# A three-stage kernel: the residual's rows are added to the Fourier stage's terms in channel mixing, on GpSimd, instead of within the Fourier stage on VectorE and GpSimd

## The chip, the cores and the metric

The kernel runs on one core of a Trainium2 chip. A core has five engines that run side by side, each with its own queue in a fixed order: TensorE (PE) for matmuls, VectorE (DVE), ScalarE (ACT) and GpSimd (POOL) for elementwise work, and SyncE (SP), which here only issues transfers (DMAs). ACT and POOL issue transfers too. An instruction that waits holds everything behind it on its queue. The metric is the time of one execution in microseconds (us), and less is better.

## The reference

Eight heads of linear attention over 8 batches of 576 rows give x of 8 x 576 x 512. A mixing layer with gates follows, and then the part that the change touches:

```python
def _moe2_ref(x, w_ch1, w_ch2):
    X = np.fft.fft(x, axis=1)
    X = np.fft.fft(X, axis=2)
    mixed = np.real(X).astype(np.float32)
    u = x + mixed
    mu = np.mean(u, axis=-1, keepdims=True)
    var = np.mean((u - mu) ** 2, axis=-1, keepdims=True)
    un = (u - mu) / np.sqrt(var + 1e-06)
    ch = np.maximum(un @ w_ch1, 0.0) @ w_ch2
    return (u + ch).astype(np.float32)
```

`x + mixed` is the residual: the rows that went into the Fourier transform are added to the real part of its result, and channel mixing (a layer norm and two matmuls) works on the sum u.

## The kernel before, in words

The program has three stages. Stage 1 (0 to 708 us) is attention and the gated mixing; it writes the rows x to `x1d` in DRAM, in 4 pairs of images (batches) of 9 tiles of 128 rows (`NTP` = 9): 4 tiles of each image, and a fifth tile of the pair that holds the last 64 rows of both.

Stage 2, the Fourier stage, goes over the 8 images. For image n, `f_load` brings 4 tiles of x into `xtt` (4 buffers) and, once for each pair, the shared tile into `xlt`. `f_eo` (L680 on VectorE, L681 on GpSimd) forms sums and differences of mirrored rows in `eot`, `f_fold` (L687, L690, L691, L697) the same of mirrored columns, split into a high and a low part in `fht`. `f_s` transforms along the rows: TensorE `pz` (L722), then `zt` (L724 on ScalarE, L725 on VectorE). `f_d` transforms along the columns in three parts m = 0, 1, 2 (128, 128 and 64 rows): TensorE `pd` (L756), a copy `bs` on ScalarE (L761), and on VectorE `wa`, whose two halves are the difference (L762) and the sum (L763). By symmetry each half serves two output tiles, once as it is and once mirrored along the columns. `acc` then adds the halves to the rows of x in place: columns 0 to 256 on VectorE (L766), columns 257 to 511 on GpSimd (L767). The sums are stored to `ud`, one store for each tile, on ACT's queue (L773, L779) and on SP's (L780). The step function `for t in range(-3, 4 * B + 1)` interleaves the images, four steps apart.

Stage 3 is channel mixing: 9 chunks c of 4 tiles of 128 rows. `u_load` brings the tiles of a chunk from `ud` into `ua` (two buffers, L820); the loads of chunk 0 wait for the last matmul of image 3 (`st["mm", 3]`). `ln` normalizes a tile: `bn` (L832), `mv` (L833 to L835), `una` (L837), transposes (L842), and `uh` and `ul` (L844, L845). For each of 16 slices f of the hidden layer `g1` forms `ph` (L853 to L855), `hh` on ScalarE (L858) and `hl` on VectorE (L859), and `g2` multiplies them with the second weight, one slice later (L900 to L902). `g2` adds the result to `ua` (L905) and stores it. During chunk 0 the two weights of each slice are loaded as raw 64-bit words (L62, four buffers) and split: L67 and L81 on ScalarE, L69, L72 and L75 on VectorE, L82 on GpSimd. The raw loads of slices 0 and 1 wait for image 4's last matmul, those of slices 2 and 3 for image 6's.

The order of the instructions on each engine is decided by a scheduler that simulates a timeline, not by hand: instructions of stages 2 and 3 are mixed where their inputs allow it, and bn of chunk 0 and the first weight splits run within the Fourier stage.

Of the kernel before, what the change touches and what calls it, by code (L numbers as in the profile page):

```python
# [10 lines left out]
F32 = mybir.dt.float32  # L11
# [10 lines left out]
D = H * DH  # L22
# [20 lines left out]
def kernel(ctx, tc, q, k, v, mu_k, mu_r, w_k, w_v, w_r, w_ch1, w_ch2, tab_s, tab_d, out):  # L43
# [1 line left out]
    const = ctx.enter_context(tc.tile_pool(name="const", bufs=1))  # L45
    dram = ctx.enter_context(tc.tile_pool(name="dram", bufs=1, space=DRAM))
    x1d = [dram.tile([NTP, P, D], F32, name=f"x1d{p}") for p in range(NPAIR)]
    ud = [dram.tile([P, D], F32, name=f"ud{i}") for i in range(NPAIR * NTP)]

    ident = const.tile([P, P], F32, name="ident")  # L50
    make_identity(nc, ident)
# [3 lines left out]
    def after(ins, to):  # L55
        tc.add_manual_dep(
            ins.ins, to, mybir.DependencyInfo(mybir.DependencyClass.Sync, mybir.DependencyReason.DATA), reason="pace"
        )
# [522 lines left out]
    with ExitStack() as ph:  # L581
# [50 lines left out]
        ts_ = p2.tile([P, 2, 2, 4, NS], F32R, name="ts_")  # L632
        td_ = p2.tile([P, 2, 2, 2, KC], F32R, name="td_")
        alt = p2.tile([P, KC], F32R, name="alt")
        NXT = 4
        xtt = [p2.tile([P, 4, D], F32, name=f"xtt{i}") for i in range(NXT)]
        nc.gpsimd.dma_start(ts_, tab_s)
        nc.gpsimd.dma_start(td_, tab_d[:, 0 : 8 * KC].rearrange("p (a b c n) -> p a b c n", a=2, b=2, c=2))
# [100 lines left out]
        def f_d(n, m):  # L739
            p, par = divmod(n, 2)  # L740
            z = st["z", n]
            cols = slice(256, 320) if m == 2 else slice(m * P, (m + 1) * P)
            w = 64 if m == 2 else P
            o = 64 * par if m == 2 else 0
            pd = [ps.tile([P, KC], F32, tag="pd", name=f"pd{n}_{m}_{ab}", bufs=4) for ab in range(2)]
            for ab in (1, 0):
                mm = []
                for dt in range(2):
                    i = 2 * ab + dt
                    mm.append((z[:, 0, i, cols], td_[:, 0, ab, dt]))  # L750
                    mm.append((z[:, 0, i, cols], td_[:, 1, ab, dt]))
                    mm.append((z[:, 1, i, cols], td_[:, 0, ab, dt]))
                if ab == 0:
                    mm.append((z256[n % 2][:, cols], alt))
                for j, (a, b) in enumerate(mm):
                    ins = nc.tensor.matmul(pd[ab][0:w], a, b, start=j == 0, stop=j == len(mm) - 1)  # L756
            st["mm", n] = ins.ins.name
            bs = p2.tile([P, KC], F32, tag="bs", name=f"bs{n}_{m}", bufs=2)
            wa = p2.tile([P, 2, KC], F32, tag="wa", name=f"wa{n}_{m}", bufs=2)
            r = slice(o, o + w)  # L760
            nc.scalar.copy(bs[0:w], pd[1][0:w])  # L761
            nc.vector.tensor_tensor(out=wa[r, 0], in0=pd[0][0:w], in1=bs[0:w], op=ALU.subtract)  # L762
            nc.vector.tensor_tensor(out=wa[r, 1], in0=pd[0][0:w], in1=bs[0:w], op=ALU.add)  # L763

            def acc(x, a, b, e0, e1):
                e0.tensor_tensor(out=x[:, 0:257], in0=x[:, 0:257], in1=wa[r, a, 0:257], op=ALU.add)  # L766
                e1.tensor_tensor(out=x[:, 257:512], in0=x[:, 257:512], in1=wa[r, b, 255:0:-1], op=ALU.add)  # L767

            if m == 2:
                xl = st["xl", p]  # L770
                acc(xl[r], 0, 1, nc.vector, nc.gpsimd)
                if par:
                    nc.scalar.dma_start(ud[p * NTP + 4], xl)  # L773
            else:
                xt = st["xt", n]
                acc(xt[:, m], 0, 1, nc.vector, nc.gpsimd)
                acc(xt[:, 2 + m], 1, 0, nc.vector, nc.gpsimd)
                i0 = p * NTP + 5 * par
                nc.scalar.dma_start(ud[i0 + m], xt[:, m])  # L779
                nc.sync.dma_start(ud[i0 + 2 + m], xt[:, 2 + m])  # L780

        for t in range(-3, 4 * B + 1):
            for n in range(B):
# [20 lines left out]
    with ExitStack() as ph:  # L804
# [7 lines left out]
        of = out.flatten_outer_dims()  # L812
        NCH = 9
        CT = 4
        us, uT = {}, {}

        def u_load(c):
            u = ua[c % 2]
            for t in range(CT):
                ld = nc.sync.dma_start(u[:, t], ud[c * CT + t])  # L820
                if c == 0:
                    after(ld, st["mm", 3])
            us[c] = u

        def ln(c, t):
            u = us[c]
            if t == 0:
                uT[c] = ((uha, ula), (uhb, ulb))[c % 2]
            uh, ul = uT[c]
            bn = top.tile([P, 6], F32, tag="bn", name="bn", bufs=2)  # L830
            mv = top.tile([P, 2], F32, tag="mv", name="mv", bufs=2)
            nc.vector.bn_stats(bn, u[:, t])  # L832
            nc.vector.bn_aggr(mv, bn)  # L833
            nc.scalar.activation(out=mv[:, 1:2], in_=mv[:, 1:2], func=AF.Sqrt, bias=eps)
            nc.vector.reciprocal(mv[:, 1:2], mv[:, 1:2])  # L835
            un = una[t % 2]
            nc.vector.tensor_scalar(  # L837
                un, u[:, t], mv[:, 0:1], mv[:, 1:2], op0=ALU.subtract, op1=ALU.mult
            )
            pt = psa.tile([P, NK, P], F32, tag="pt", name="pt", bufs=1)  # L840
            for kt in range(NK):
                nc.tensor.transpose(pt[:, kt], un[:, kt * P : (kt + 1) * P], ident)  # L842
            cs = slice(t * P, (t + 1) * P)
            nc.scalar.copy(uh[:, :, cs], pt)  # L844
            nc.vector.tensor_tensor(out=ul[:, :, cs], in0=pt, in1=uh.bitcast(F32)[:, :, cs], op=ALU.subtract)  # L845
# [151 lines left out]
```

## Time and profile before

| what | value |
|---|---|
| median of 3 runs | 1672.5 us (1672.42 to 1673.82) |
| the profiled execution | 1676.39 us |
| its span, first to last instruction | 1674.6 us (1.8 us lie around it) |
| mean granted TensorE clock | 0.971 of full speed |
| busy: PE, DVE, ACT, POOL | 1548.0, 746.7, 594.9, 491.5 us |
| Fourier stage | about 708 to 836 us |
| chunk 0 of channel mixing | 836 to 946 us |

The time of the profiled execution is compared with a view of the same execution alone; it lies 3.9 us above the median of the runs. The share of busy time is an average over stages with different limits, so a stage is read by itself: which engine is full there, and what the others wait for. Durations of matmuls overlap, since they are pipelined.

### The profile page before, as it was taken

What the parts mean: (1) busy time and instruction counts of PE and PEld (TensorE: products, weight loads), DVE (VectorE), ACT (ScalarE), POOL (GpSimd) and SP (SyncE); (2) the same over time, 40 slices, a digit from 0 to 9 for tenths busy, and PEclk for the clock granted to TensorE, in tenths of its full rate; (3) what the DMA queues carried; (4) which work ended last, traced back from release to release, by engine and by line L of the source; (5) the groups of instructions that cost most, each with busy time, mean ns of one, the idle gap of its engine ahead of it and who ended that gap; (6) DMA issues with size and microseconds to landing.
All of it is one profiled execution on the core that took longest, in us unless ns stands there. A gap on an engine that the chain in (4) does not pass through costs nothing.

```text
span 1674.6 us, 19835 instructions
## 1 busy us (share of the span) xinstructions
PE 1548.0 (92%) x7560; PEld 1313.2 (78%) x7560; DVE 746.7 (45%) x1342; ACT 594.9 (36%) x1120; POOL 491.5 (29%) x532
## 2 busy tenths in 40 slices
PE   2497999899989999987887999999999999999998
PEld 2476899788879888776765888888888888888886
DVE  7966544645365442199999312212221313131211
ACT  4673666566556564233445111111111111111110
POOL 4464663646365555265445000000000000000000
PEclk9598999999999999988999999999999999999999
DMA  7521322222212101435454101001010101010000
GB/s 196 164 83 51 85 56 68 64 56 70 69 51 63 58 13 51 170 110 196 167 192 157 51 0 41 11 1 50 1 51 1 50 1 51 0 51 1 26 0 26
DMA packets 117863, 108.91 MB, mean 65 GB/s; under 512 B 54760, under 2 KB 91752, under 8 KB 117512
## 3 DMA queue, kind: packets, MB, share of 16 engines
q1 hardware_dynamic: 107736, 84.37, 17.1%
q10 hardware_dynamic: 8064, 14.68, 2.4%
q0 software_dynamic: 1968, 8.60, 1.4%
q8 instruction: 59, 0.97, 0.2%
q14 instruction: 36, 0.29, 0.1%
HBM read 79.31 MB, written 28.31 MB: 64 GB/s over the span
## 4 chain that ended last, share of the span: by engine, by line
PE 66%; DVE 12%; issue 10%; POOL 4%; ACT 4%; DMA 3%; SPq 1%; POOLq 0%; ACTq 0%; DVEq 0%
PE ph L853 6%; PE ph L855 6%; PE pc L900 6%; PE ph L854 6%; PE pc L902 6%; PE pc L901 6%; PE pv L469 3%; PE pv L470 3%; PE pv L471 3%; PE pk L438 3%; PE pk L439 3%; PE pk L440 3%; DVE xm L416 2%; PE pr L454 1%; PE pr L455 1%
## 5 line engine op out<-in xcount | busy, mean ns | idle before, releaser
L859 DVE SCALAR_TENSOR_TENSOR hl<-ph,hh 128x512 fp32r<-128x512 f32 x144 | 99.2, 689 | 443.8 <-ACT hh L858 443.8
L858 ACT ACTIVATE hh<-ph 128x512 fp32r<-128x512 f32 x144 | 85.9, 597 | 515.3 <-PE ph L855 515.3
L884 POOL DMA_INDIRECT out_dram<-ua,rev x16 | 15.7, 979 | 732.0 <-DVE ua L905 731.6
L902 PE MATMUL pc<-w2h,hl 128*128 128x512 f32 x576 | 222.9, 393 | 8.2 <-DVE hl L859 8.2
L900 PE MATMUL pc<-w2h,hh 128*128 128x512 f32 x576 | 226.5, 393 | 3.9 <-ACT hh L858 3.9
L901 PE MATMUL pc<-w2l,hh 128*128 128x512 f32 x576 | 224.8, 390 | 0.0
L416 DVE SCALAR_TENSOR_TENSOR xm<-dt,omu,xb 128x63 f32<-128x63 f32 (+4 forms) x224 | 115.7, 566 | 83.2 <-POOL xr_lo L425 35.0
L438 PE MATMUL pk<-xk_hi,wk_hi 128*128 128x384 f32 x384 | 131.0, 350 | 12.4 <-ACT xk_hi L424 11.4
L446 POOL TENSOR_TENSOR kk_lo<-h,kk_hi 128x384 fp32r<-128x384 f32 x96 | 98.8, 1033 | 148.6 <-ACT h L445 130.7
L902 PEld LDWEIGHTS pc<-w2h,hl 128*128 128x128 f32 x576 | 107.6, 188 | 35.3 <-DVE hl L859 11.6
L439 PE MATMUL pk<-xk_lo,wk_hi 128*128 128x384 f32 x384 | 131.4, 343 | 0.2 <-POOL xk_lo L425 0.2
L900 PEld LDWEIGHTS pc<-w2h,hh 128*128 128x128 f32 x576 | 108.1, 188 | 29.9 <-ACT hh L858 6.5
L853 PE MATMUL ph<-uha,w1h 128*128 128x512 f32 x320 | 127.7, 401 | 2.8 <-ACT w1h L81 2.8
L440 PE MATMUL pk<-xk_hi,wk_lo 128*128 128x384 f32 x384 | 130.1, 340 | 0.0
L855 PE MATMUL ph<-uha,w1l 128*128 128x512 f32 x320 | 127.3, 398 | 1.2 <-POOL w1l L82 1.2
L854 PE MATMUL ph<-ula,w1h 128*128 128x512 f32 x320 | 126.8, 396 | 0.0
L901 PEld LDWEIGHTS pc<-w2l,hh 128*128 128x128 f32 x576 | 108.2, 188 | 23.6
L469 PE MATMUL pv<-wv,kk_hi 128*128 128x512 f32 x288 | 113.1, 394 | 0.6 <-ACT sgt L458 0.6
L470 PE MATMUL pv<-wv,kk_hi 128*128 128x512 f32 x288 | 112.9, 394 | 0.0
L471 PE MATMUL pv<-wv,kk_lo 128*128 128x512 f32 x288 | 112.4, 393 | 0.0
L853 PE MATMUL ph<-uhb,w1h 128*128 128x512 f32 x256 | 100.9, 397 | 0.0
L855 PE MATMUL ph<-uhb,w1l 128*128 128x512 f32 x256 | 100.0, 391 | 0.0
(206 smaller groups left out, 3178.6 us busy)
## 6 DMA issues: line engine op xcount, KB each, us to landing
raw<-in_moe_w_ch_dram SPq DMA_DIRECT2D x32, 512.0 KB
x1d<-sgt ACTq DMA_DIRECT2D x36, 256.0 KB
ua<-ud SPq DMA_DIRECT2D x36, 256.0 KB
kt<-in_k_dram SPq DMA_DIRECT2D x32, 256.0 KB
xtt<-x1d SPq DMA_DIRECT2D x8, 1024.0 KB
vt<-in_v_dram SPq DMA_DIRECT2D x60, 128.0 KB
qtT<-in_q_dram SPq DMA_DIRECT2D x8, 512.0 KB
qtB<-in_q_dram SPq DMA_DIRECT2D x8, 512.0 KB
```

The lines of the kernel that those rows point to most:

```text
L438: nc.tensor.matmul(pk, wh, xk_hi[:, kt], start=kt == 0, stop=False)
L439: nc.tensor.matmul(pk, wh, xk_lo[:, kt], start=False, stop=False)
L440: mm = nc.tensor.matmul(pk, wl, xk_hi[:, kt], start=False, stop=kt == NK - 1)
L469: nc.tensor.matmul(pv, kk_hi[f][:, ts], wv_hi[f // 2][:, f % 2], start=f == 0, stop=False)
L470: nc.tensor.matmul(pv, kk_hi[f][:, ts], wv_lo[f // 2][:, f % 2], start=False, stop=False)
L471: mm = nc.tensor.matmul(pv, kk_lo[f][:, ts], wv_hi[f // 2][:, f % 2], start=False, stop=f == NF1 - 1)
L853: nc.tensor.matmul(ph_, w1h[f][:, kt], uh[:, kt], start=kt == 0, stop=False)
L854: nc.tensor.matmul(ph_, w1h[f][:, kt], ul[:, kt], start=False, stop=False)
L855: nc.tensor.matmul(ph_, w1l[f][:, kt], uh[:, kt], start=False, stop=kt == NK - 1)
L900: nc.tensor.matmul(a, hh[:, cs], w2h[f], start=f == 0, stop=False)
L901: nc.tensor.matmul(a, hh[:, cs], w2l[f], start=False, stop=False)
L902: nc.tensor.matmul(a, hl[:, cs], w2h[f], start=False, stop=f == NF2 - 1)
```

## The change

The Fourier stage no longer adds the rows of x. `f_d` stores `wa` as it is, both halves in one transfer, to new buffers in DRAM: `wad` for m = 0 and 1 (128 x 2 x 258, 258 KB each), `wal` for m = 2 (64 rows of it). All 24 stores are on SP's queue. In channel mixing `u_load` brings the tile of x from `x1d` into `ua` and the `wa` that belongs to it into a new tile `wl` (4 buffers); `u_add`, called at the head of `ln`, adds the two halves to the rows on GpSimd. A `wa` of m = 0 or 1 serves two tiles and is loaded twice. `xtt` has 3 buffers instead of 4, the loads of chunk 0 wait for image 1's last matmul instead of image 3's, and the buffer for the descriptors of transfers that GpSimd issues is set to 4096 bytes.

```diff
--- before.py
+++ after.py
@@ -45,7 +45,9 @@
     const = ctx.enter_context(tc.tile_pool(name="const", bufs=1))
     dram = ctx.enter_context(tc.tile_pool(name="dram", bufs=1, space=DRAM))
     x1d = [dram.tile([NTP, P, D], F32, name=f"x1d{p}") for p in range(NPAIR)]
-    ud = [dram.tile([P, D], F32, name=f"ud{i}") for i in range(NPAIR * NTP)]
+
+    wad = [[dram.tile([P, 2, KC], F32, name=f"wad{n}_{m}") for m in range(2)] for n in range(B)]
+    wal = [dram.tile([P, 2, KC], F32, name=f"wal{p}") for p in range(NPAIR)]
 
     ident = const.tile([P, P], F32, name="ident")
     make_identity(nc, ident)
@@ -632,7 +634,7 @@
         ts_ = p2.tile([P, 2, 2, 4, NS], F32R, name="ts_")
         td_ = p2.tile([P, 2, 2, 2, KC], F32R, name="td_")
         alt = p2.tile([P, KC], F32R, name="alt")
-        NXT = 4
+        NXT = 3
         xtt = [p2.tile([P, 4, D], F32, name=f"xtt{i}") for i in range(NXT)]
         nc.gpsimd.dma_start(ts_, tab_s)
         nc.gpsimd.dma_start(td_, tab_d[:, 0 : 8 * KC].rearrange("p (a b c n) -> p a b c n", a=2, b=2, c=2))
@@ -762,22 +764,10 @@
             nc.vector.tensor_tensor(out=wa[r, 0], in0=pd[0][0:w], in1=bs[0:w], op=ALU.subtract)
             nc.vector.tensor_tensor(out=wa[r, 1], in0=pd[0][0:w], in1=bs[0:w], op=ALU.add)
 
-            def acc(x, a, b, e0, e1):
-                e0.tensor_tensor(out=x[:, 0:257], in0=x[:, 0:257], in1=wa[r, a, 0:257], op=ALU.add)
-                e1.tensor_tensor(out=x[:, 257:512], in0=x[:, 257:512], in1=wa[r, b, 255:0:-1], op=ALU.add)
-
             if m == 2:
-                xl = st["xl", p]
-                acc(xl[r], 0, 1, nc.vector, nc.gpsimd)
-                if par:
-                    nc.scalar.dma_start(ud[p * NTP + 4], xl)
+                nc.sync.dma_start(wal[p][r], wa[r])
             else:
-                xt = st["xt", n]
-                acc(xt[:, m], 0, 1, nc.vector, nc.gpsimd)
-                acc(xt[:, 2 + m], 1, 0, nc.vector, nc.gpsimd)
-                i0 = p * NTP + 5 * par
-                nc.scalar.dma_start(ud[i0 + m], xt[:, m])
-                nc.sync.dma_start(ud[i0 + 2 + m], xt[:, 2 + m])
+                nc.sync.dma_start(wad[n][m], wa)
 
         for t in range(-3, 4 * B + 1):
             for n in range(B):
@@ -812,18 +802,31 @@
         of = out.flatten_outer_dims()
         NCH = 9
         CT = 4
-        us, uT = {}, {}
+        us, uT, wl = {}, {}, {}
 
         def u_load(c):
             u = ua[c % 2]
             for t in range(CT):
-                ld = nc.sync.dma_start(u[:, t], ud[c * CT + t])
+                p, j = divmod(c * CT + t, NTP)
+                ld = nc.sync.dma_start(u[:, t], x1d[p][j])
                 if c == 0:
-                    after(ld, st["mm", 3])
+                    after(ld, st["mm", 1])
+                w = top.tile([P, 2, KC], F32, tag="wl", name=f"wl{c}_{t}", bufs=4)
+                nc.sync.dma_start(w, wal[p] if j == 4 else wad[2 * p + j // 5][j % 5 % 2])
+                wl[c, t] = w
             us[c] = u
+
+
+        def u_add(c, t):
+            w, x = wl.pop((c, t)), us[c][:, t]
+            j = (c * CT + t) % NTP
+            a = 1 if j != 4 and j % 5 >= 2 else 0
+            nc.gpsimd.tensor_tensor(out=x[:, 0:257], in0=x[:, 0:257], in1=w[:, a, 0:257], op=ALU.add)
+            nc.gpsimd.tensor_tensor(out=x[:, 257:512], in0=x[:, 257:512], in1=w[:, 1 - a, 255:0:-1], op=ALU.add)
 
         def ln(c, t):
             u = us[c]
+            u_add(c, t)
             if t == 0:
                 uT[c] = ((uha, ula), (uhb, ulb))[c % 2]
             uh, ul = uT[c]
@@ -975,7 +978,7 @@
     from concourse import mybir as _mybir
     from concourse.bass_utils import run_bass_kernel_spmd as _run
 
-    nc = _bacc.Bacc("TRN2", target_bir_lowering=False, num_devices=1)
+    nc = _bacc.Bacc("TRN2", target_bir_lowering=False, num_devices=1, dynamic_dma_scratch_size=4096)
     arrays, args = {}, []
     tab_s, tab_d = _tables()
     for name, a in [(n, inputs[n]) for n in _INS] + [("tab_s", tab_s), ("tab_d", tab_d)]:
```

Line numbers of the kernel after the change are higher by two up to L766 and by three behind the loads of `ua`; L766 and L767 are gone, and `u_add` is L824 and L825.

VectorE, at image 2 before the change (the names carry buffer numbers; `xtt_6354` is the x of image 2, and `wa_0` and `wa_1` are its first two tiles):

```order
L762 TENSOR_TENSOR wa_0_6746<-pd_0_0_6730,bs_0_6745 128x258
L763 TENSOR_TENSOR wa_0_6746<-pd_0_0_6730,bs_0_6745 128x258
L762 TENSOR_TENSOR wa_1_6779<-pd_1_0_6763,bs_1_6778 128x258
L763 TENSOR_TENSOR wa_1_6779<-pd_1_0_6763,bs_1_6778 128x258
L725 TENSOR_TENSOR zt_6337<-pz_0_1_6823,zt_6337 128x320
L766 TENSOR_TENSOR xtt_6354<-xtt_6354,wa_0_6746 128x257
L737 TENSOR_TENSOR z_6360<-pz_r,z_6360 2x320
L766 TENSOR_TENSOR xtt_6354<-xtt_6354,wa_0_6746 128x257
L766 TENSOR_TENSOR xtt_6354<-xtt_6354,wa_1_6779 128x257 x2
L680 TENSOR_TENSOR eot_6338<-xtt_6353 128x1024
```

After the change, from image 1's last two `wa` tiles to image 2's first (L764 and L765 are the two halves of wa, L835 is bn, L682 eot, L727 zt, L689 to L693 fold):

```order
L689 TENSOR_TENSOR fold_6323<-eot_6322 128x2x255
L693 TENSOR_TENSOR fold_6323<-eot_6322 128x2x255
L764 TENSOR_TENSOR wa_2_6627<-pd_2_0_6611,bs_2_6626 64x258
L765 TENSOR_TENSOR wa_2_6627<-pd_2_0_6611,bs_2_6626 64x258
L727 TENSOR_TENSOR zt_6321<-pz_0_0_6760,zt_6321 128x320
L692 COPY fold_6323<-eot_6322 128x2x2
L835 BN_STATS bn<-ua_6296 128x6
L727 TENSOR_TENSOR zt_6321<-pz_0_1_6772,zt_6321 128x320
L682 TENSOR_TENSOR eot_6322<-xtt_6337 128x1024
L739 TENSOR_TENSOR z_6343<-pz_r,z_6343 2x320
L835 BN_STATS bn<-ua_6296 128x6
```

The adds L766 are gone from between the `wa` and the folds, and the first bn of chunk 0 has moved ahead, from behind image 3's last `wa` to right behind image 1's.

VectorE, where image 6 ends and the first weights of slice 2 are split, before the change:

```order
L762 TENSOR_TENSOR wa_1_7349<-pd_1_0_7333,bs_1_7348 128x258
L763 TENSOR_TENSOR wa_1_7349<-pd_1_0_7333,bs_1_7348 128x258
L762 TENSOR_TENSOR wa_2_7375<-pd_2_0_7359,bs_2_7374 64x258
L763 TENSOR_TENSOR wa_2_7375<-pd_2_0_7359,bs_2_7374 64x258
L766 TENSOR_TENSOR xtt_6354<-xtt_6354,wa_1_7349 128x257 x2
L725 TENSOR_TENSOR zt_6337<-pz_1_1_7426,zt_6337 128x320
L766 TENSOR_TENSOR xlt_6348<-xlt_6348,wa_2_7375 64x257
L69 TENSOR_SCALAR raw<-raw 128x512
L72 SCALAR_TENSOR_TENSOR raw<-raw 128x512
L762 TENSOR_TENSOR wa_0_7454<-pd_0_0_7438,bs_0_7453 128x258
L763 TENSOR_TENSOR wa_0_7454<-pd_0_0_7438,bs_0_7453 128x258
```

After the change (L71, L74 and L77 are the splits' steps L69, L72 and L75 of before):

```order
L764 TENSOR_TENSOR wa_2_7279<-pd_2_0_7263,bs_2_7278 64x258
L765 TENSOR_TENSOR wa_2_7279<-pd_2_0_7263,bs_2_7278 64x258
L727 TENSOR_TENSOR zt_6321<-pz_1_1_7329,zt_6321 128x320
L71 TENSOR_SCALAR raw<-raw 128x512
L74 SCALAR_TENSOR_TENSOR raw<-raw 128x512
L77 SCALAR_TENSOR_TENSOR raw<-raw 128x512
L71 TENSOR_SCALAR raw<-raw 128x512
L764 TENSOR_TENSOR wa_0_7357<-pd_0_0_7341,bs_0_7356 128x258
L765 TENSOR_TENSOR wa_0_7357<-pd_0_0_7341,bs_0_7356 128x258
```

Between image 6's last `wa` and the first raw step there were a pair of adds, a zt and another add; one zt is left.

SP's queue in the Fourier stage, before the change, from the first stores of image 0 and 1 (`xtt_6352` and `xtt_6353`) on:

```order
L780 DMA ud_66<-xtt_6352 128x512
L780 DMA ud_67<-xtt_6352 128x512
L660 DMA xtt_6352<-x1d_62 128x4x512
L780 DMA ud_71<-xtt_6353 128x512
L780 DMA ud_72<-xtt_6353 128x512
L820 DMA ua_6313<-ud_69 128x512
L820 DMA ua_6313<-ud_71 128x512
L660 DMA xtt_6353<-x1d_62 128x4x512
L820 DMA ua_6313<-ud_70 128x512
```

After the change, from the last `wa` of image 0 on (`ua_6296` is chunk 0's buffer, the `wl` with numbers from 7780 are chunk 1's, `wl_0_8492` is chunk 2's first):

```order
L768 DMA wal_80<-wa_2_6493 64x516
L770 DMA wad_0_66<-wa_0_6578 128x516
L811 DMA ua_6296<-x1d_60 128x512 x4
L770 DMA wad_1_67<-wa_1_6606 128x516
L768 DMA wal_80<-wa_2_6627 64x516
L815 DMA wl_0_7780<-wal_80 128x516
L815 DMA wl_1_7783<-wad_0_66 128x516
L770 DMA wad_0_68<-wa_0_6706 128x516
L815 DMA wl_2_7786<-wad_1_67 128x516
L770 DMA wad_1_69<-wa_1_6734 128x516
L815 DMA wl_3_7789<-wad_0_66 128x516
L815 DMA wl_0_8492<-wad_1_67 128x516
```

Stores of `ud` have given way to stores of `wa`, and loads of `wl` stand between them; each such load needs its `wa` stored and its buffer read by the `u_add` of a chunk before.

## Rows read from the trace of the kernel before

**Rows 1.** Page: busy us (share) xinstructions by engine; chain by engine.

```profile
PE 1548.0 (92%) x7560; PEld 1313.2 (78%) x7560; DVE 746.7 (45%) x1342; ACT 594.9 (36%) x1120; POOL 491.5 (29%) x532
...
PE 66%; DVE 12%; issue 10%; POOL 4%; ACT 4%; DMA 3%; SPq 1%; POOLq 0%; ACTq 0%; DVEq 0%
```

**Rows 2.** Stretches: bounds, length, busy us of each engine, PEclk, DMA share, GB/s.

```profile
705.00:836.00 131.00, 104.77 (x681) 96.21 (x680) 121.74 (x208) 46.19 (x103) 74.46 (x74) 0.91 0.45 158
836.00:946.00 110.00, 93.88 (x389) 71.30 (x388) 85.82 (x112) 45.94 (x76) 44.99 (x33) 0.98 0.43 138
780.00:800.00 20.00, 17.72 (x117) 16.58 (x117) 19.78 (x41) 8.96 (x20) 9.66 (x9) 0.87 0.44 148
920.00:940.00 20.00, 20.00 (x90) 16.05 (x89) 3.63 (x6) 3.15 (x6) 2.02 (x2) 1.00 0.00 1
1100.00:1668.00 568.00, 567.06 (x2513) 463.41 (x2511) 128.46 (x230) 78.39 (x143) 11.28 (x12) 1.00 0.07 21
```

**Rows 3.** VectorE's groups, Fourier stage: shapes, count, us, mean ns, idle.

```profile
L766 DVE TENSOR_TENSOR xtt<-xtt,wa 128x257 f32<-128x257 f32 x28 | 17.7, 668 | 0.0
...
L697 DVE TENSOR_TENSOR fht<-fold,fht 128x1032 fp32r<-128x1032 f32 x7 | 12.8, 1828 | 1.8 <-ACT fht L696 1.7
L687 DVE TENSOR_TENSOR fold<-eot 128x510 f32<-128x510 f32 x8 | 11.5, 1439 | 0.1
...
L762 DVE TENSOR_TENSOR wa<-pd,bs 128x258 f32<-128x258 f32 x16 | 6.6, 415 | 0.0
...
L766 DVE TENSOR_TENSOR xlt<-xlt,wa 64x257 f32<-64x257 f32 x7 | 3.5, 500 | 0.1
```

**Rows 4.** TensorE's groups in the Fourier stage, the first.

```profile
L722 PE MATMUL pz<-ts__6349,fht 128*128 128x320 f32 x192 | 48.9, 343 | 16.1 <-DVE zt L725 9.8 <-ACT fht L696 6.2
```

**Rows 5.** Tile xtt: count, ns min/median/max, first and last start.

```profile
L767 POOL TENSOR_TENSOR xtt<-xtt,wa x32: 627/736/1390, 738.9 to 837.9; 128x255 f32<-128x255 f32 x32
L766 DVE TENSOR_TENSOR xtt<-xtt,wa x32: 397/422/2585, 740.2 to 839.6; 128x257 f32<-128x257 f32 x32
...
L681 POOL TENSOR_TENSOR eot<-xtt x8: 2332/2536/3382, 711.3 to 787.5; 128x1024 f32<-128x1024 f32 x8
```

**Rows 6.** Chain of waits in the Fourier stage: start us, us, what.

```profile
710.24 1.10 DVE fold L687
...
727.58 2.77 DVE fold L687
...
742.81 2.66 DMA ud<-xtt
...
745.61 6.37 DMA xtt<-x1d
...
828.46 5.21 DMA raw<-in_moe_w_ch_dram
```

**Rows 7.** VectorE's groups in chunk 0.

```profile
L75 DVE SCALAR_TENSOR_TENSOR raw<-raw 128x512 int32<-128x512 int32 x28 | 28.8, 1033 | 0.3
L72 DVE SCALAR_TENSOR_TENSOR raw<-raw 128x512 int32<-128x512 int32 x27 | 23.6, 878 | 0.9
L69 DVE TENSOR_SCALAR raw<-raw 128x512 int32<-128x512 int32 x27 | 21.0, 776 | 1.3 <-DMA raw<-in_moe_w_ch_dram 1.3
```

**Rows 8.** Timeline, image 6's end: start, us, engine, line [idle before <-releaser].

```profile
833.69 0.43 DVE L69 TENSOR_SCALAR raw<-raw 128x512 int32<-128x512 int32 x1 [1.07 <-DMA raw<-in_moe_w_ch_dram]
```

**Rows 9.** Timeline at the Fourier stage's start.

```profile
708.98 1.22 DVE L680 TENSOR_TENSOR eot<-xtt 128x1024 f32<-128x1024 f32 x1
```

**Rows 10.** Timelines of VectorE and TensorE in channel mixing.

```profile
1134.96 0.69 DVE L859 SCALAR_TENSOR_TENSOR hl<-ph,hh 128x512 fp32r<-128x512 f32 x1 [2.17 <-ACT hh L858]
1136.64 0.69 DVE L832 BATCH_NORM_STATS2 bn<-ua 128x6 f32<-128x512 f32 x1 [0.98 <-DMA ua<-ud]
...
1146.07 0.69 DVE L859 SCALAR_TENSOR_TENSOR hl<-ph,hh 128x512 fp32r<-128x512 f32 x1 [3.62 <-ACT hh L858]
...
1140.11 0.40 PE L902 MATMUL pc<-w2h,hl 128*128 128x512 f32 x1
```

## The prediction

> **What bounds the kernel now.** I read the page's busy line and its chain first, then busy time by stretch, then the costliest groups of the stretches where TensorE is not full. TensorE is busy 92% of the span and holds 66% of the chain, VectorE (DVE) 12% [rows 1]. The average hides three different limits [rows 2]. In channel mixing after its first chunk TensorE works 567.06 of 568 us: nothing on another engine can shorten that stretch, only a new stall can change it, for the worse. In the Fourier stage (705 to 836 us) TensorE works 104.77 of 131 us while VectorE works 121.74, and in a typical slice 19.78 of 20. In chunk 0 (836 to 946 us) VectorE works 85.82 us, nearly all of it before 920 us: from 920 to 940, with the weights split, it is down to 3.63 and TensorE at 20.00 of 20. So from about 709 us [rows 9] to about 920 us the time is VectorE's queue, image work first and weight splits behind it, and an instruction taken out of that queue moves the end until TensorE is the bound itself. TensorE's largest idle in the stage is 16.1 us ahead of the first transform, 9.8 of it ended by VectorE's zt and 6.2 by the start [rows 4].
>
> **What is taken away.** VectorE loses 32 adds of 128x257 (28 of them before 836 us, 17.7 us, mean 668 ns) and 8 of 64x257 (7 of them, 3.5 us, mean 500 ns) [rows 3]: 32 x 0.668 + 8 x 0.500 = 25.4 us of a full queue. But the mean is not the work: the fastest such add takes 397 ns, the median 422, the longest 2585 [rows 5]. The long ones lie beside a GpSimd (POOL) subtraction L681 of 2332 to 3382 ns, and so does the fold L687, which takes 1.10 us at 710 us and 2.77 at 727 [rows 5, 6]. With the adds gone, L681 (8 times) stays, and what it slowed down in an add it can slow down in the next VectorE instruction. At medians the 40 adds are 40 x 0.422 = 16.9 us. So the bounds for VectorE are 16.9 and 25.4 us; I take 21, halfway: of GpSimd's work beside VectorE the subtractions L681 stay and the adds L767 go.
>
> GpSimd loses as many adds (median 736 ns [rows 5], 40 x 0.74 = 29 us). It is busy 74.46 of 131 us [rows 2], so it did not bound anything, but its work collides. It gets 72 of the same adds back, of which 16 (chunks 0 and 1, 12 us) fall within the Fourier stage by the order, and the other 56 in channel mixing. Net 17 us less GpSimd work beside VectorE's. The 8.5 us by which the 40 adds exceed their median stand against 74 us of GpSimd work, and the other groups have such an excess too (L697 1828 ns and L687 1439 ns on average [rows 3]); at 0.12 us of loss for each us of GpSimd, 17 x 0.12 = 2 us more are won. Zero is the lower bound; the upper, if the rest of VectorE's groups lose twice as much as the adds did, 6 us.
>
> The Trainium skill (GPSIMD Engine Reference, section 1) says that GpSimd shares its SBUF interfaces with VectorE and contends with VectorE instructions that have two SBUF inputs. The long adds and folds beside L681 agree. By this rule the adds' whole excess could move to the folds, which have two SBUF inputs as well; the sum would then stand on 16.9 instead of 21 us, 4 us less gain. The same page (section 3.1) has GpSimd 1.96 times as slow as VectorE in such an add, which speaks against moving VectorE's half there; in this trace the ratio of medians is 736 to 422, or 1.74 [rows 5].
>
> **What is added, in the Fourier stage.** (1) Instead of 36 stores of rows the kernel issues 24 stores of wa, all on SP's queue. VectorE could refill one of the two wa buffers once GpSimd's add had read it; now it has to wait until the store has landed. The nearest row is a ud store of the same size, 2.66 us [rows 6]. Two wa tiles in a row need the buffer of two before; by the order most of them stand apart by zt, fold or fht instructions (L687 1.4, L697 1.8 us [rows 3]). I take 2 us in sum (some 0.3 to 0.6 us where an image's third tile comes early); the bounds are 0 and, if each of the 24 waits one us, 24. (2) The first bn of chunk 0 comes to stand behind image 1's last wa. Its rows are loaded only once image 1's last matmul has run, and then come a load (2.66 us) and two GpSimd adds (2 x 0.74 = 1.5). From that matmul to bn VectorE has two wa halves of 0.42 us [rows 3] and waits for the copy ahead of them, which I put at another 0.5: about 1.4 us. So it stalls 2.66 + 1.5 - 1.4 = 2.8, say 3 us. The third and fourth bn wait on GpSimd's queue, where eot L681 (2.5 us) lies between the adds: 1 us each. In sum 5. Behind the stalled bn on VectorE's queue stand zt and eot, for which TensorE waits. If loads land late among the other transfers (1 MB took 6.37 us [rows 6]) it is 9. (3) Where image 6 ends, four adds stood as filler while the first raw weights of slice 2 landed: load 5.21 us [rows 6], VectorE idle for only 1.07 us [rows 8]. These adds are in the 21 us, but the load, released by the same last matmul, does not land sooner for want of them: 2.7 us come back as idle time (4 x 0.42 us of work at medians and about 1 for their collisions). (4) At the stage's start the first xtt load now stands behind the loads of image 0's other rows on a queue that waits for the last x1d store; it is needed at 708.98 [rows 9]. It may be late by 0 to 2 us; I take 1.
>
> **What is added, in channel mixing.** 36 loads of 258 KB more and 36 pairs of GpSimd adds. GpSimd is idle there, and bytes are not scarce. The wl load of a chunk is issued a chunk early, so what changes is that each bn waits 1.5 us longer than its row's load, and the four follow each other at 1.5 us on GpSimd. In the group shown, bn starts at 1136.64; two to three bn stand in VectorE's order ahead of the next hl, so bn's third would end at 1136.64 + 3 x 1.5 + 0.7 = 1141.8 and hl at 1142.5. The hl of the time before, started 1134.96, is used by TensorE (L902) at 1140.11; the second hl after it starts at 1146.07, so the slices follow at (1146.07 - 1134.96) / 2 = 5.5 us, and the late hl is needed at 1145.6 [rows 10]. Some 3 us of slack are left: cost 0. The cover is TensorE's own work on hh (L900, L901), which stands ahead of L902.
>
> **The sum.** -21 - 2 + 2 + 5 + 2.7 + 1 = -12.3 us, rounded to -13 because the xtt buffers now come free at eot instead of at the store (2.66 + 6.37 us in the chain at 742 us [rows 6]) and let a fold start a little sooner. All of it passes through chunk 0, since its splits are the same queue: L69, L72 and L75 take 73.4 us there [rows 7]. On the profiled execution 1676.4 - 13 = 1663.4; the median of the runs is 3.9 us lower, 1672.5, and so the forecast is 1659.5. Own range, from the bounds of the adds (16.9 or 25.4), 2 us of collisions and the stalls (8 to 14): a gain of 5 to 19 us, 1653 to 1667.
>
> **The rivals.** A: VectorE's whole price comes back, collisions too, and stalls are filled by work that had to be done anyway: 25.4 + 2 - 3 = 24 us, 1648. TensorE's 26 us of idle time [rows 2] are the ceiling. For it: VectorE has no idle time of its own there to be lost. Against it: the new waits are in its own queue. B: the waits in the Fourier stage eat most of it: SP's queue holds wa stores behind wl loads that wait for GpSimd's adds (the first wl load of chunk 1 waits for chunk 0's first add, and image 2's stores stand behind it), so that each of some 12 wa tiles waits 1 us: gain 13 - 12 = 1, 1671. For it: SP is in order, and the piece of its queue shown above mixes both. C, on the other side: in channel mixing hl stands behind a bn whose add is late. From about 3 us of lateness beyond what I computed, each us is a us of TensorE: a load that lands late among stores of the output, as where bn waits longest, would cost 3 us in each of 7 chunks, 21 us, against 13 won: 1680. It decides from 2 us a chunk. For it: bn waits for its load even now; against it: the loads and adds have 3 us of slack, and wl is there a chunk early.
>
> **How the numbers follow.** Forecast's own case 0.58, A 0.15, B 0.15, C 0.12. The range is 1648 to 1671: it leaves out C and the half of A that wins more than reckoned, about 0.2. A measurement of this kernel can tell about 0.2%, 3.3 us; faster by more than that (below 1669.2) takes in the forecast's case, A, and a third of B, 0.78; within it the rest of B, 0.10; slower C alone, 0.12.
>
> **What would show it.** Right: VectorE's adds are gone and VectorE's full stretch, now up to 920 us, ends 10 to 16 us sooner, with TensorE idle 10 to 15 us less between 705 and 946; VectorE idle 3 us at the first bn, ended by GpSimd; channel mixing after chunk 0 as long as now, TensorE idle under 2 us. Wrong: VectorE's idle ahead of wa ended by a DMA adding up to over 6 us (B), or TensorE waiting for hl in each chunk (C), or folds as slow as before beside L681 with the adds' 8.5 us gone to them.

## The result and the profile after

The kernel after takes 1658.76 us (median of 4 runs, 1655.99 to 1659.42), the one before 1672.87 (1672.42 to 1673.82): ratio 0.9912, 95% interval 0.9895 to 0.9929, so 14 us faster. A second set of runs gave 0.9907 (0.9891 to 0.9924); below, 0.991 is taken for it, and one thousandth is 1.67 us. Forecast were 1659.5 us and a range of 1648 to 1671.

Busy time by stretch of the kernel after (bounds, length, busy us of PE, PEld, DVE, ACT and POOL with counts, granted clock, DMA share, GB/s), beside [rows 2]:

```profile
705.00:836.00 131.00, 106.70 (x713) 97.62 (x712) 114.03 (x188) 51.66 (x112) 65.91 (x58) 0.95 0.56 185
836.00:946.00 110.00, 97.46 (x416) 75.67 (x415) 77.42 (x103) 42.22 (x71) 42.63 (x33) 1.00 0.40 129
...
1100.00:1650.00 550.00, 549.54 (x2443) 450.93 (x2441) 126.56 (x225) 76.32 (x139) 37.78 (x51) 1.00 0.09 29
```

VectorE still works most of the Fourier stage, but has gaps now. TensorE is full in channel mixing as before, with GpSimd's adds beside it. VectorE's groups of the Fourier stage, beside [rows 3]; the first line is eot before:

```profile
L680 DVE TENSOR_TENSOR eot<-xtt 128x1024 f32<-128x1024 f32 x8 | 11.2, 1396 | 0.3 <-DMA xtt<-x1d 0.3
...
L682 DVE TENSOR_TENSOR eot<-xtt 128x1024 f32<-128x1024 f32 x8 | 19.2, 2403 | 2.1 <-DMA xtt<-x1d 2.1
L727 DVE TENSOR_TENSOR zt<-pz,zt 128x320 fp32r<-128x320 f32 x32 | 15.1, 480 | 2.8 <-ACT zt L726 2.7
L699 DVE TENSOR_TENSOR fht<-fold,fht 128x1032 fp32r<-128x1032 f32 x7 | 10.7, 1533 | 1.2 <-ACT fht L698 1.2
L689 DVE TENSOR_TENSOR fold<-eot 128x510 f32<-128x510 f32 x8 | 7.1, 888 | 0.1
```

The adds are gone, and another group has grown: eot (L680, now L682) takes 2403 ns instead of 1396, 8.0 us more in all, and 1208 at the median with GpSimd's half of it moved away (experiment eot_vec). The fold (L687, now L689) has shrunk from 1439 to 888 ns. So GpSimd's collisions have moved from the adds and folds to eot: the adds' 8.5 us above their median are about what eot has gained. The timelines show why. Before, VectorE's half of eot started first, and GpSimd's half took longer; after, GpSimd's starts just ahead of VectorE's, or alone. Before:

```profile
731.34 1.21 DVE L680 TENSOR_TENSOR eot<-xtt 128x1024 f32<-128x1024 f32 x1
731.50 3.30 POOL L681 TENSOR_TENSOR eot<-xtt 128x1024 f32<-128x1024 f32 x1 [1.70 <-DVE fold L691]
```

After:

```profile
748.18 2.41 POOL L683 TENSOR_TENSOR eot<-xtt 128x1024 f32<-128x1024 f32 x1 [3.43 <-DVE fold L693]
...
750.93 1.20 DVE L682 TENSOR_TENSOR eot<-xtt 128x1024 f32<-128x1024 f32 x1
...
754.71 2.41 POOL L683 TENSOR_TENSOR eot<-xtt 128x1024 f32<-128x1024 f32 x1 [4.12 <-DVE fold L692]
755.02 3.18 DVE L682 TENSOR_TENSOR eot<-xtt 128x1024 f32<-128x1024 f32 x1
```

Where the time went is read best between fixed points of the program. Stage 1 ends at slightly different times from profile to profile (705.5 to 709.0 us, with the same instructions), so the table counts from the start of its last matmul (L471 before, L473 after). The columns are the starts of the first transform (pz), of the last pd, of the last weight split's last step on VectorE (L75, L77 after), of the first matmul of chunk 1 (ph of uhb), and the time from that to the last matmul of the same line in chunk 7, nearly 7 chunks. The chip's time is the ratio to the kernel before.

| kernel | first pz | last pd | last split | chunk 1 | 7 chunks | ratio, interval |
|---|---|---|---|---|---|---|
| before | 6.5 | 128.3 | 211.0 | 237.9 | 625.9 | 1 |
| after | 9.3 | 120.4 | 195.1 | 224.6 | 623.9 | 0.9912 (0.9895 to 0.9929) |
| vec_back | 9.7 | 124.4 | 205.1 | 234.6 | 624.0 | 0.9967 (0.9955 to 0.9978) |
| pool_back | 9.6 | 123.3 | 202.2 | 231.7 | 624.1 | 0.9948 (0.9933 to 0.9962) |
| both_back | 9.8 | 133.9 | 211.7 | 241.3 | 623.8 | 1.0012 (1.0003 to 1.0020) |
| before_no_vec | 6.5 | 119.0 | 198.5 | 224.5 | 625.9 | 0.9911 (0.9896 to 0.9927) |
| gate01 | 6.6 | 113.8 | 191.2 | 220.7 | 624.0 | 0.9877 (0.9860 to 0.9894) |
| wa3 | 10.4 | 118.1 | 194.1 | 222.2 | 624.0 | 0.9889 (0.9875 to 0.9904) |
| gate3 | 9.9 | 121.4 | 197.9 | 231.3 | 624.0 | 0.9941 (0.9928 to 0.9953) |
| slow_add | 10.8 | 120.6 | 196.4 | 225.9 | 624.1 | 0.9906 (0.9893 to 0.9920) |
| after_again | 10.0 | 119.7 | 194.4 | 224.0 | 624.0 | 0.9907 (0.9891 to 0.9924) |
| gate01_low | 6.5 | 114.0 | 191.2 | 218.1 | 624.0 | 0.9873 (0.9857 to 0.9890) |
| gate01_wa3 | 6.6 | 113.8 | 189.2 | 218.6 | 624.0 | 0.9876 (0.9859 to 0.9892) |
| eot_vec | 8.7 | 110.3 | 187.5 | 219.1 | 623.9 | 0.9873 (0.9857 to 0.9890) |

From before to after the last split comes 15.9 us sooner, chunk 1 13.3 us, and the seven chunks behind it save another 2.0; from chunk 1 to the end of the span it is 2.9 us (1674.6 - 945.8 before, 1656.6 - 930.7 after). From stage 1's last matmul to about 1 us behind the last split VectorE's time divides so, first before, then after:

```profile
707.90:920.60 212.70, 170.35 (x942) 144.51 (x941) 202.72 (x312) 88.39 (x172) 117.61 (x104) 0.94 0.50 167
```

```profile
706.10:902.90 196.80, 159.97 (x930) 137.03 (x929) 178.29 (x269) 87.31 (x170) 100.57 (x80) 0.97 0.55 180
```

VectorE's work is down by 202.72 - 178.29 = 24.4 us, and its idle time up from 212.70 - 202.72 = 10.0 to 196.80 - 178.29 = 18.5 us. Of the 43 instructions fewer 40 are the adds; the other three (an una, an hl and an ulb, some 2 us) come behind the last split now. What it waited for, most first (us in total, times, longest), before:

```profile
DVE sgt L475 <- PE pv L471: 4.8, 1, 4.8
DVE fht L697 <- ACT fht L696: 3.1, 4, 1.1
DVE raw L69 <- DMA raw<-in_moe_w_ch_dram: 2.3, 3, 1.1
...
DVE raw L72 <- ACT raw L67: 0.3, 1, 0.3
```

After:

```profile
DVE sgt L477 <- PE pv L473: 4.8, 1, 4.8
DVE zt L727 <- ACT zt L726: 2.7, 4, 1.0
DVE raw L71 <- DMA raw<-in_moe_w_ch_dram: 2.5, 3, 1.6
DVE raw L74 <- ACT raw L73: 2.3, 2, 2.1
DVE eot L682 <- DMA xtt<-x1d: 2.1, 1, 2.1
DVE ulb L848 <- ACT uhb L847: 1.3, 1, 1.3
DVE fht L699 <- ACT fht L698: 1.2, 2, 0.7
DVE wa L764 <- ACT bs L763: 0.9, 1, 0.9
...
DVE raw L74 <- ACT raw L69: 0.5, 2, 0.3
...
DVE wa L764 <- DMA wad<-wa: 0.3, 1, 0.3
```

No bn stands in this list, and the wait for wa's stores is 0.3 us in all. The first wait is there before, too.

TensorE gains in two ways. Up to chunk 1's first matmul, before, then after:

```profile
707.90:945.80 237.90, 195.55 (x1055) 164.98 (x1054) 207.56 (x319) 92.13 (x178) 119.02 (x105) 0.94 0.45 150
706.10:930.70 224.60, 187.77 (x1054) 159.73 (x1053) 185.24 (x279) 92.14 (x178) 102.00 (x81) 0.97 0.48 158
```

Of the 13.3 us only 42.35 - 36.83 = 5.5 are idle time; 7.8 are busy time of the same matmuls, at a granted clock of 0.97 instead of 0.94. The clock is a rival to VectorE's queue, and the traces speak against it as the cause: TensorE still waits for hl or hh until just before or just behind the start of the last split, 919.51 us before and 899.50 after, so most of what it did faster ahead of that wait turned into waiting; before_no_vec, below, agrees. Behind it TensorE is full, at a clock of 1.00 in both:

```profile
919.50:945.80 26.30, 26.29 (x117) 21.09 (x118) 5.52 (x9) 4.73 (x8) 2.52 (x2) 1.00 0.00 1
899.50:930.70 31.20, 31.20 (x141) 25.52 (x142) 9.30 (x13) 6.50 (x11) 3.49 (x3) 1.00 0.00 1
```

### The profile page after: what moved, and what is told of

Its sections match the earlier page's. It is cut to its first block, busy times and chain, and to the rows that moved or that the text cites. A ratio compares the mean times of both kernels' runs of the same rounds, so it can differ in the third digit from the quotient of the medians.

```text
span 1656.6 us, 19891 instructions
## 1 busy us (share of the span) xinstructions
PE 1537.8 (93%) x7560; PEld 1309.2 (79%) x7560; DVE 728.3 (44%) x1302; ACT 595.3 (36%) x1120; POOL 511.7 (31%) x564
## 4 chain that ended last, share of the span: by engine, by line
PE 42%; issue 7%; DVE 1%; POOL 1%; DMA 1%; ACT 0%; POOLq 0%; DVEq 0%; ACTq 0%; SPq 0%
PE ph L856 7%; PE ph L857 7%; PE ph L858 7%; PE pc L905 7%; PE pc L904 7%; PE pc L903 7%; DMA raw<-in_moe_w_ch_dram 1%; PE pt L845 1%; POOL w1l L84 1%; POOL w2l L84 1%; PE pd L758 1%; PE pz L724 1%; DVE raw L74 0%; DVE raw L71 0%; ACT raw L69 0%
## 5 line engine op out<-in xcount | busy, mean ns | idle before, releaser
L887 POOL DMA_INDIRECT out_dram<-ua,rev x16 | 15.9, 991 | 667.3 <-DVE hl L862 311.4
L440 PE MATMUL pk<-xk_hi,wk_hi 128*128 128x384 f32 x384 | 130.0, 347 | 11.7 <-ACT xk_hi L426 10.7
L471 PE MATMUL pv<-wv,kk_hi 128*128 128x512 f32 x288 | 113.1, 394 | 0.7 <-ACT sgt L460 0.7
L473 PE MATMUL pv<-wv,kk_lo 128*128 128x512 f32 x288 | 112.4, 393 | 0.0
```

Of the source, the lines that this page charges most:

```text
L440: nc.tensor.matmul(pk, wh, xk_hi[:, kt], start=kt == 0, stop=False)
L471: nc.tensor.matmul(pv, kk_hi[f][:, ts], wv_hi[f // 2][:, f % 2], start=f == 0, stop=False)
```

## The experiments

Names in bold are those of the table.

**vec_back, pool_back, both_back** put the removed work back, each engine's alone and both, on a scratch tile behind the wa stores:

```diff
+            for a in (0,) if m == 2 else (0, 1):
+                nc.vector.tensor_tensor(out=scr[r, 0:257], in0=scr[r, 0:257], in1=wa[r, a, 0:257], op=ALU.add)
+            for a in (0,) if m == 2 else (0, 1):
+                nc.gpsimd.tensor_tensor(out=scr[r, 257:512], in0=scr[r, 257:512], in1=wa[r, 1 - a, 255:0:-1], op=ALU.add)
```

> The kernel after, with 40 VectorE adds put back behind the wa tiles, of the shapes that were taken away (32 of 128x257, 8 of 64x257), but on a scratch tile, so that they change no result and hold no buffer but wa. Theory (VectorE's queue is the bound): these cost 17 to 22 us, so the time is 1676 to 1681, at or above the time of the kernel before, since its new waits stay. Rival (the gain comes from the structure: xtt buffers freed early, no store before the next load, chunk 0's rows loaded early): VectorE has idle gaps for them, under 5 us, 1659 to 1664.

> The kernel after, with 40 GpSimd adds put back behind the wa tiles (32 of 128x255, 8 of 64x255), on a scratch tile. Theory: GpSimd is not the bound and its adds only slow VectorE where they lie beside it, 2 to 4 us, 1661 to 1663. Rival (GpSimd's relief, by the collisions with VectorE, is most of the gain): 8 us or more, 1667 and up.

> The kernel after with both sets of adds put back on the scratch tile: 40 on VectorE and 40 on GpSimd. Alone they cost 9 to 10 us (VectorE) and 6 to 7 us (GpSimd). Theory (the whole gain is this work taken from the Fourier stage, adds and their collisions): the sum or a little more, 16 to 20 us, so the time of the kernel before within 4 us, ratio 0.998 to 1.003. Rival (part of the gain is the structure: buffers freed early, early loads): the two overlap, under 12 us, ratio under 0.996.

VectorE's adds cost (0.9967 - 0.991) x 1674 = 9.5 us, between theory and rival; GpSimd's 6.4 us, over the theory and near the rival; both together 17 us, about their sum, and that theory held. The same stretch as above, to the last split, for vec_back, pool_back and both_back:

```profile
708.70:915.50 206.80, 165.11 (x930) 140.58 (x929) 192.97 (x309) 88.41 (x170) 102.37 (x82) 0.93 0.53 173
```

```profile
707.80:911.70 203.90, 164.99 (x930) 139.40 (x929) 183.88 (x269) 87.52 (x170) 135.00 (x122) 0.95 0.55 176
```

```profile
705.50:917.80 212.30, 167.22 (x923) 141.47 (x922) 198.29 (x309) 86.99 (x168) 135.21 (x122) 0.93 0.53 169
```

VectorE's adds are 192.97 - 178.29 = 14.7 us of work, of which 4.7 go into its gaps (idle 18.5 to 13.8). GpSimd's adds are no VectorE work, and yet VectorE is busy 183.88 - 178.29 = 5.6 us longer: the collisions. But pool_back puts back more than the change took away: GpSimd is busy 135.00 us, 34.4 more than after and 17.4 more than before, since `u_add` of chunks 0 and 1 stays. By the change's own relief, 117.61 - 100.57 = 17.0 us, the 6.4 us would be 3.2, an estimate in proportion. With both back the kernel is 2 us slower than before. Chunk 1 then starts 3.4 us later than before, and channel mixing wins the 2.0 us as in the kernel after. In the same proportion GpSimd's surplus is worth 3.2 us of it, so by this estimate what else the change moves neither gains nor costs much ahead of chunk 1.

**before_no_vec** takes VectorE's adds alone out of the kernel before (columns 0 to 256 of the transform are left out of u):

```diff
-                e0.tensor_tensor(out=x[:, 0:257], in0=x[:, 0:257], in1=wa[r, a, 0:257], op=ALU.add)
```

> The kernel before without the 40 VectorE adds L766: columns 0 to 256 of the transform's result are left out of u, all else (stores, buffers, GpSimd's adds) stays. Theory: 17 to 25 us faster than before, 1648 to 1656, which is the whole price of the adds without the new waits. Rival (the structure): the stores and the next xtt load still follow each other, so 5 us or less, 1668 to 1673.

14.9 us, a little under the theory's lowest and far over the rival's 5. So the queue carries it, also with the stores and buffers of before. To the last split, and to chunk 1:

```profile
706.10:906.30 200.20, 168.42 (x948) 144.57 (x947) 177.87 (x272) 87.68 (x172) 116.99 (x105) 0.94 0.54 178
706.10:930.60 224.50, 192.72 (x1055) 164.33 (x1054) 182.72 (x279) 91.40 (x178) 118.03 (x105) 0.95 0.48 158
```

VectorE's work falls by 202.72 - 177.87 = 24.8 us, nearly the whole price by the mean, and its idle time rises from 10.0 to 22.3: half of the freed time is lost to waits. TensorE is busy only 2.8 us less than before up to chunk 1, and chunk 1 comes 13.4 us sooner all the same, as in the kernel after: the gain does not need the shorter busy time.

**gate01** restores the order at the head of SP's queue, by letting the loads of chunk 1's rows wait for image 1 as well; **wa3** gives wa a third buffer; **gate01_wa3** does both:

```diff
-                if c == 0:
+                if c < 2:
                     after(ld, st["mm", 1])
...
-            wa = p2.tile([P, 2, KC], F32, tag="wa", name=f"wa{n}_{m}", bufs=2)
+            wa = p2.tile([P, 2, KC], F32, tag="wa", name=f"wa{n}_{m}", bufs=3)
```

> The kernel after, with the loads of chunk 1's rows made to wait for image 1's last matmul as those of chunk 0 do, so that the first xtt load is the first on SP's queue again. In the kernel after the first transform starts 9.3 us after stage 1's last matmul, in the one before 6.5. Theory: the start is on the path, so 2 to 3 us faster than after, 1656. Rival: what VectorE does later anyway fills it, no change, 1658 to 1660.

> The kernel after with three wa buffers instead of two, so that VectorE hardly waits for a wa store to land. Theory (that wait is 0.3 us in the trace after): no change, within 2 us of after, ratio 0.990 to 0.993. Rival (the two buffers hold VectorE and TensorE back where the trace names another releaser): 4 us or more faster, ratio under 0.989.

> The kernel gate01 with three wa buffers. By the two runs alone it would be 5.8 + 3.7 us faster than after, ratio 0.9855. Theory (both only let VectorE's queue run without gaps, and the wait for wa stores is 0.2 us in gate01's trace): within 2 us of gate01, 0.9865 to 0.989.

gate01 wins 5.5 us, twice the theory. The rows of the start, after and gate01:

```profile
709.35 3.40 DVE L682 TENSOR_TENSOR eot<-xtt 128x1024 f32<-128x1024 f32 x1 [2.06 <-DMA xtt<-x1d]
...
715.40 0.90 PE L724 MATMUL pz<-ts__6333,fht 128*128 128x320 f32 x2 [8.92 <-ACT fht L698]
```

```profile
707.36 1.22 DVE L682 TENSOR_TENSOR eot<-xtt 128x1024 f32<-128x1024 f32 x1
...
709.72 2.33 POOL L683 TENSOR_TENSOR eot<-xtt 128x1024 f32<-128x1024 f32 x1
709.81 2.27 DVE L692 COPY fold<-eot 128x4 f32<-128x4 f32 x1
...
712.79 0.90 PE L724 MATMUL pz<-ts__6333,fht 128*128 128x320 f32 x2 [6.15 <-ACT fht L698]
```

The late load costs 2.06 us of waiting. Then eot takes 3.40 us instead of 1.22, since GpSimd's half, which waits for the same load, starts at the same time. But gate01 pays for GpSimd's half too, in a small copy that takes 2.27 us (0.17 in the kernel after), so from eot to pz it wins only 0.6 us, 5.43 instead of 6.05. The table has 2.7 us at the first pz and 3.9 at chunk 1; the rest of the 5.5 lies within what two medians differ by. wa3 wins 3.5 us by its median, more than the theory's 2 and less than the rival's 4, with intervals that overlap; on top of gate01 it gives nothing, as expected. Whether wa's stores cost the kernel after more than the 0.3 us in its trace is not settled.

**gate3** lets chunk 0's loads wait for image 3 again, as before the change:

```diff
-                    after(ld, st["mm", 1])
+                    after(ld, st["mm", 3])
```

> The kernel after with the loads of chunk 0's rows made to wait for image 3's last matmul, as before the change, instead of image 1's. Theory (VectorE has the same work in another order, and TensorE is not waiting for chunk 0's layer norm): within 3 us of after, ratio 0.989 to 0.993. Rival (the early layer norm of chunk 0 fills VectorE's gaps or spares a wait at the end of the stage): 4 us or more slower than after, ratio over 0.994.

It is 5.2 us slower: the rival by its numbers. But the cause is not shown. In the profiled execution (1668.11 us, the slowest of six) the last split is 2.8 us later and chunk 1 6.7. Up to chunk 1, and behind TensorE's last wait:

```profile
709.00:940.30 231.30, 194.95 (x1055) 165.87 (x1054) 184.98 (x279) 92.47 (x178) 97.36 (x81) 0.93 0.48 155
908.30:940.30 32.00, 32.00 (x137) 25.93 (x138) 6.78 (x10) 5.26 (x10) 1.31 (x1) 0.95 0.00 1
```

TensorE is busy 7.2 us longer than after on the same matmuls and idle no longer (36.35 us), at a granted clock of 0.93 instead of 0.97; and behind its last wait, where all of its time counts, the clock is 0.95 instead of 1.00. So the longer busy time covers all of the 6.7 us, and the share of the early layer norm stays open.

**slow_add** doubles GpSimd's work ahead of bn in chunks 2 to 8, the cost that my rival C was about:

```diff
+            if c > 1:
+                nc.gpsimd.tensor_tensor(out=scr[:, 0:257], in0=x[:, 0:257], in1=w[:, a, 0:257], op=ALU.add)
+                nc.gpsimd.tensor_tensor(out=scr[:, 257:512], in0=x[:, 257:512], in1=w[:, 1 - a, 255:0:-1], op=ALU.add)
```

> The kernel after with GpSimd's work for each tile of chunks 2 to 8 doubled (each pair of adds is done once more into a scratch tile first), so that bn comes 1.35 us later for the first and up to 5 us later for the fourth tile. Theory (hl has some 3 us of slack ahead of L902): with two or three bn ahead of hl it is 2.7 to 4 us later, so most chunks lose nothing and some 1 us: 0 to 7 us slower than after, ratio 0.991 to 0.996. Rival (each us of lateness costs TensorE a us, as in my rival C): 7 chunks x 3 to 4 us, 20 us or more, ratio over 1.003.

No change, 624.1 us for the seven chunks. Its timeline shows why (L839 bn, L866 hl; the waits are for GpSimd's second add):

```profile
1127.53 0.69 DVE L839 BATCH_NORM_STATS2 bn<-ua 128x6 f32<-128x512 f32 x1 [4.44 <-POOL ua L829]
...
1128.36 0.66 DVE L866 SCALAR_TENSOR_TENSOR hl<-ph,hh 128x512 fp32r<-128x512 f32 x1
1130.39 0.70 DVE L839 BATCH_NORM_STATS2 bn<-ua 128x6 f32<-128x512 f32 x1 [0.62 <-POOL ua L829]
```

With the longer adds the scheduler has put this hl behind the first bn of its group, in the kernel after it stands behind the third; so this run doesn't show where lateness begins to cost, only that this much GpSimd work is free in the order that the scheduler makes of it.

**eot_vec** moves GpSimd's half of eot to VectorE:

```diff
-            nc.gpsimd.tensor_tensor(out=eo[:, 1], in0=xt[:, 0:2], in1=xt[:, 2:4], op=ALU.subtract)
+            nc.vector.tensor_tensor(out=eo[:, 1], in0=xt[:, 0:2], in1=xt[:, 2:4], op=ALU.subtract)
```

> The kernel after with GpSimd's half of eot (L683, 8 subtractions of 2.38 us) moved to VectorE, where such an operation alone takes 1.2 us: 9.7 us more work in VectorE's queue, and 19 us less of GpSimd beside it. VectorE's own half takes 2403 ns on average in the kernel after, 1.2 us when alone. Theory (the time beyond 1.2 us is lost to GpSimd's half beside it, 8 x 1.2 = 9.6 us): the two cancel, within 3 us of after, ratio 0.989 to 0.993. Rival (GpSimd's work beside it costs VectorE little): 7 us or more slower, ratio over 0.995.

6.2 us faster than after, on the other side of the rival and beyond the theory. The two halves, both on VectorE, take together what one took beside GpSimd (count, ns min/median/max, first and last start):

```profile
L682 DVE TENSOR_TENSOR eot<-xtt x8: 1184/1208/1648, 710.2 to 779.4; 128x1024 f32<-128x1024 f32 x8
```

```profile
L683 DVE TENSOR_TENSOR eot<-xtt x8: 1204/1210/1505, 711.7 to 765.9; 128x1024 f32<-128x1024 f32 x8
```

```profile
706.70:896.00 189.30, 157.96 (x919) 135.04 (x918) 174.79 (x277) 86.24 (x169) 76.17 (x72) 0.96 0.59 189
```

With eight instructions more in its queue VectorE is busy 174.79 us, 3.5 less than after, and idle 14.5 instead of 18.5 (in a window that ends 0.7 us nearer to the last split).

**gate01_low** takes 14 of the splits' shifts (L71) off VectorE and gives them to ScalarE; **after_again** is the base line:

```diff
-                split64(raw, hi, lo, f >= 2)
+                split64(raw, hi, lo, f >= 2 and f % 2)
```

> The kernel gate01 with one step of the weight split (the shift L71 of slices 2 to 15) moved from VectorE to ScalarE for every second slice: 14 instructions of 0.73 us, 10 us less in VectorE's queue, 14 more on ScalarE, which is busy 88 of 193 us. Theory (VectorE's queue is still the bound, up to the last split): 4 to 9 us faster than gate01, ratio 0.982 to 0.985. Rival (TensorE or the loads have become the bound): under 2 us, ratio 0.986 to 0.989.

> The kernel after once more, unchanged, on the chip of the runs beside it, as the base line for them: ratio 0.990 to 0.993.

The rival held: 1653.20 us, gate01's time. VectorE has 177.81 - 168.71 = 9.1 us less work up to the last split than in gate01, and the last split comes at 191.2 us all the same. gate01_low's stretch, and what waited in its chunk 0:

```profile
707.40:900.40 193.00, 164.44 (x942) 142.12 (x941) 168.71 (x257) 95.90 (x185) 99.16 (x80) 0.96 0.59 186
```

```profile
ACT raw L69 <- DMA raw<-in_moe_w_ch_dram: 11.3, 15, 1.5
...
DVE raw L71 <- DMA raw<-in_moe_w_ch_dram: 4.5, 5, 2.0
DVE raw L74 <- ACT raw L73: 3.4, 4, 1.4
```

VectorE now waits for raw weights, which have four buffers that GpSimd's last step frees. So with the start mended VectorE's queue is no longer what bounds chunk 0; that the buffers' round trip is, was argued from these waits and not tried.

## Why the prediction was right

**VectorE's queue as the bound** is shown, by adds put back (9.5 us) and by adds taken out of the kernel before (14.9 us). It bounds as far as the last split; gate01_low shows where that ends.

**The adds and their collisions** were put at 21 + 2 = 23 us of VectorE's time; the work is down 24.4 to the last split, and 207.56 - 185.24 = 22.3 to chunk 1, where both kernels have the same instructions but for the 40 adds. The split was off: VectorE's adds are 14.7 us of work and 9.5 us of time where they are put back (forecast 16.9 to 25.4), GpSimd's relief is some 3 us by the estimate above (forecast 2, upper bound 6). The 25.4 us by mean duration contained GpSimd's collisions, as the prediction said; they did move, but to eot (8.0 us), not to the folds, which have become shorter.

**The stalls** were put at 10.7 us and are 8.5 us, but not where I had them. bn behind image 1's last wa: forecast 5, measured 0.1; VectorE came there late enough for the loads and adds to be done, and the order's queue alone doesn't tell that. wa's stores: forecast 2, traced 0.3. The start: forecast 1, measured 2.8. The raw weights: forecast 2.7 more for the load, which is 2.5 against 2.3 before; instead VectorE waits 2.8 us for ScalarE's steps on them (L73, L69), 0.3 before. Waits of zt, ulb and wa for ScalarE, 4.9 us, were not forecast: they stand in the trace where VectorE's queue is no longer full. The 0.7 us that the sum gives to xtt's buffers no run tests alone.

**All of it passes through chunk 0**: nearly. Of 15.9 us at the last split 13.3 reach chunk 1, as TensorE has 29.5 us of work left there instead of 26.9.

**TensorE's idle time** between 705 and 946 us was to fall by 10 to 15 us, a sign of being right. It fell by 5.5 only (from the first two lines of [rows 2] and of the stretches above); the other part of chunk 1's 13.3 us is shorter busy time, which the prediction did not think of.

**Channel mixing at cost 0**: right on rival C. In the trace after, bn waits 25.8 us in 13 waits for GpSimd and TensorE loses nothing. The 2.9 us won from chunk 1 on were not forecast.

**Rivals.** A (24 us) needed the stalls to be filled; they were not. B's waits for stores did not come. The early load of chunk 0's rows, which I counted as a stall alone, may be worth up to 5 us (gate3), with the clock as another candidate.

So the sum was right partly by luck, as errors cancelled: too much for bn and the stores, too little for the start and the waits for ScalarE, and 2.9 us won in channel mixing against 2.6 lost behind the last split.

## What to carry to other kernels

Busy time taken out of a full queue is not the gain: here 24.8 us of VectorE's work taken out gave 14.9 us, and 14.7 us put back cost 9.5, about six tenths both times, because waits fill the rest. A mean duration mixes an instruction's own work with what the neighbour engine's instructions do to it, and the latter moves to whatever stands there next. Look at what a removed gate lets to the head of an in-order queue: the ungated loads of a later stage cost 5.5 us, and gating them gave a faster kernel (0.9877), as did an engine's work moved to the busier engine (eot_vec, 0.9873); the two together were not tried.

## What the runs showed of the hardware

The two halves of eot, on VectorE and on GpSimd, ran as if the later one waited for the earlier one's end when they met. In the kernel after, five of the eight eot of VectorE start 0.03 to 1.2 us behind GpSimd's half (2.34 to 2.41 us), and each ends 1.08 or 1.09 us after that has ended, whatever its start: 755.02 + 3.18 = 758.20 against 754.71 + 2.41 = 757.12; alone it took 1.20. Before, in the three that met, VectorE's started first by 0.1 to 0.4 us and took 1.21 to 1.52 us, and GpSimd's took 3.30 to 3.38. A copy of 128x4 beside GpSimd's half took 2.27 us in gate01, 0.17 without; not so a zt, which reads pz from PSUM: it took 0.48 us at 753.14 us in the kernel before, in the midst of GpSimd's half. So which half starts first decided whose time grew, and VectorE with eight instructions more and GpSimd with eight fewer (eot_vec) was faster.

The seven chunks of channel mixing, with the same matmuls and no idle TensorE in the trace, take 625.9 us in both kernels built on the one before and 623.8 to 624.1 in all others, 0.3 us for each chunk. In the odd chunks it lies in the first 75 matmuls, which take 393.1 ns on average before and 389.0 after. I have no cause for it.

The granted clock up to chunk 1 was 0.94 before and 0.97 after, TensorE's busy time 195.55 and 187.77 us for 1055 and 1054 matmuls. Behind its last wait it was 1.00 in both.
